# A spectral mixer feeding a squared-ReLU MLP: one scheduling block, ordered by a timeline, around the whole kernel body

## The chip, the cores and the metric

The kernel runs on one core of one Trainium2 chip. The metric is the device time of that core in microseconds (us); 838.69 us is the median of three runs of the kernel before (837.92 to 840.66).

## What is computed

Eight sequences of 3008 rows by 256 columns pass through a spectral layer and then, row by row, through an MLP of width 2048. Cut to what matters:

```python
X = np.fft.rfft(x, axis=1)                      # x: 8 x 3008 x 256
Yr = Xr @ w_r - Xi @ w_i + b_r
Yi = Xr @ w_i + Xi @ w_r + b_i
Y = shrink(Yr, 0.01) + 1j * shrink(Yi, 0.01)    # sign(v) * max(|v| - 0.01, 0)
y = np.fft.irfft(Y, n=3008, axis=1)             # as 24064 rows x 256
r = np.maximum(y @ w_in, 0.0)                   # w_in: 256 x 2048
out = (s * (r * r) + b) @ w_out                 # w_out: 2048 x 256
```

## The kernel before

**The spectral half, one batch at a time.** 3008 is 94 x 32, so each Fourier transform is done in two steps of matmuls with tables. A batch b from 1 to 7 passes four stages, each cut into small units:

- `s1_units` (L619): 16 matmuls by the first table (`A_t`, tile names `psf<-x,A_t`). Each result is copied out of PSUM into `u`, stored to DRAM (`ud`), and read back in another layout (`us`, four loads).
- `s23_units` (L649): 12 rounds of forward table (`fwd_unit`, `psf<-F_t,us`), mixing with the weights (`sum_unit` and `mix_unit`, `W_t` and `W_g`), shrinking on DVE (`shrink`, three operations L714 to L716), moving quarters between partitions (L725, 32 KB DMAs issued by SP, for the last two rounds DVE copies, L727), and the inverse table (`inv_unit`, `psf<-ring,T_t`). The results are copied into `v`, stored to DRAM (`vd`, L744, six stores), and read back as two halves (`vs`, L755).
- `s4_units` (L777): 64 matmuls of 94 columns by the last table (`psf<-C_t,vs`), in 14 groups of up to five. Each group fills one PSUM buffer of the pool `psf` (two buffers) and is copied out by ACT or DVE into `yt` (L187 or L189).

Batch 0 goes through `first_batch` (L409) without the way through DRAM.

**The MLP half, tile by tile.** `yt` is cut into 47 tiles of up to 512 rows (`_tile_order`, L73). For each of the 16 slices of the width, `first_mm` (L851) multiplies by `w_in`; two slices share a double PSUM buffer (`psh`, two of them). ACT applies the ReLU (L871, `rt<-psh`), and ACT or DVE squares it into `gt` (L881 or L884). The product with `w_out` follows one tile later: `second_mms` (L922) with 16 accumulating matmuls per 128 rows, or `seven_mms` (L983), which forms a 2x2 block product from seven products; sums of its operands are made on DVE (`s_op`, L965, L980) and by an accumulating DMA (L973), and DVE combines the results (`add`, L1011 to L1012). Results leave through `ost` by SP's stores.

**What orders the work.** The body emits everything by hand. A dictionary `plan` (L1082 to L1131) gives each unit of the next batches a slot among the 47 x 16 slots of the MLP's loop (L1134 to L1146): in each slot stand the planned units, one `first_mm` and a sixteenth of the previous tile's second product. For instance, stage 4 of batch b is spread over 13 or 14 slots that start 15 (or 14) slots ahead of that batch's own first tile:

```python
        schedule(s2 - 15 + (p < 90), 14 - (p < 90), s4_units(b))
...
                for u in plan.pop(ti * MC + mc, []):
                    u()
                first_mm(ti, mc)
...
            for u in nxt[mc]:
                u()
```

Which of ACT and DVE takes a copy or a square is decided while the body is emitted, by running loads (`evac`, L183; `act_first`, L180). The order in which SP and POOL issue DMAs also follows the emission. In a few places `tc.issue_after` ties instructions to others on their engine.

Of the kernel before, what the change touches and what calls it, by code (L numbers as in the profile page):

```python
# [96 lines left out]
def kernel(  # L97
# [11 lines left out]
    out: bass.AP,  # L109
):  # L110
    nc = tc.nc
    B, S, D = x.shape
    N = S
    assert N == N1 * N2 and D == 2 * P and B % 2 == 0
# [1063 lines left out]
```

## Time and profile before

| | before |
|---|---|
| median of 3 runs | 838.69 us |
| span of the profiled execution | 837.9 us |
| the run nearest to that span | 837.92 us |
| PE busy, share of the span, matmuls | 822.6 us, 98%, 7662 |
| ACT busy | 723.0 us, 86% |
| DVE busy | 706.9 us, 84% |
| POOL busy | 86.2 us, 10% |
| bytes moved by DMA | 107.17 MB, mean 128 GB/s |

The span runs from the first to the last instruction of the program; the execution around it adds next to nothing here. Two things help in reading. A matmul's duration in the trace includes its way through the array, so that neighbours overlap: what a matmul occupies PE for is the distance from its start to the next one's. And a row like `L871 ACT ACTIVATE rt<-psh ... x328 | 336.1, 1026 | 54.4 <-PE psh L175 52.6` says that 328 operations of that form were busy for 336.1 us, 1026 ns each, and that ACT sat idle for 54.4 us ahead of them, 52.6 of these until a matmul into `psh` was done.

### The profile page before, as it was taken

To read this page: it belongs to the slowest core of one execution; us is meant where nothing else is said; L and a number is where in the kernel's file an instruction comes from. 1 tells how busy PE (TensorE), PEld (TensorE's weight loads), DVE (VectorE), ACT (ScalarE), POOL (GpSimd) and SP (SyncE) were. 2 spreads that over 40 slices of the span, in tenths; PEclk is the share of its full clock that TensorE was granted. 3 is DMA by queue.
4 is the path that set the end of the run, shared out by engine and by line. 5 is a ranking of instruction groups with operands and counts; after the bars stand their busy time and mean duration, and the time that the engine had idled before them with its cause. 6 is when DMAs were issued, how large, how long until landed. Compare 5 with 4: busy or idle time off the path is not lost.

```text
span 837.9 us, 19547 instructions
## 1 busy us (share of the span) xinstructions
PE 822.6 (98%) x7662; PEld 600.7 (72%) x7662; DVE 706.9 (84%) x1104; ACT 723.0 (86%) x962; POOL 86.2 (10%) x114
## 2 busy tenths in 40 slices
PE   8999999999999999999999999999999999999997
PEld 7857767777677767777677676767767777767765
DVE  5888989978898888988889888797889988889885
ACT  4998988998899989998889988989889988788882
POOL 4540001100011001100011000100001000001000
PEclk8999999999999999999999999999999999999999
DMA  8954578345873378444773368723565333513321
GB/s 196 180 153 103 124 189 203 63 94 133 198 185 65 94 184 208 114 104 128 195 185 69 88 147 208 175 63 105 127 178 138 67 100 93 137 45 77 72 65 60
DMA packets 116670, 107.17 MB, mean 128 GB/s; under 512 B 12774, under 2 KB 100842, under 8 KB 115234
## 3 DMA queue, kind: packets, MB, share of 16 engines
q1 hardware_dynamic: 102498, 80.55, 33.6%
q0 software_dynamic: 14080, 25.37, 19.1%
q8 instruction: 60, 0.98, 0.5%
q14 instruction: 32, 0.26, 0.1%
HBM read 53.52 MB, written 46.66 MB: 120 GB/s over the span
## 4 chain that ended last, share of the span: by engine, by line
PE 75%; DVE 12%; ACT 6%; DMA 3%; issue 3%; SPq 0%; POOL 0%; DVEq 0%; POOLq 0%
PE psh L175 31%; PE psa L175 28%; PE psf L175 16%; ACT rt L871 3%; DVE gt L884 2%; DVE gt L980 2%; ACT gt L881 1%; DVE ring L699 1%; PE psm L175 1%; DMA gt<-gt 1%; DVE ost L1012 1%; DMA ring<-ring 1%; DVE s L980 1%; DMA x<-in_x_dram 1%; DVE zz L1012 1%
## 5 line engine op out<-in xcount | busy, mean ns | idle before, releaser
L871 ACT ACTIVATE rt<-psh 128x1024 f32<-128x1024 f32 (+2 forms) x384 | 386.7, 1008 | 57.0 <-PE psh L175 55.1
L175 PEld LDWEIGHTS <-gt 128*128 128x128 f16 (+1 forms) x3696 | 304.8, 101 | 167.7 <-DMA gt<-gt 0.5
L175 PE MATMUL psh<-yt,w_in 128*128 128x512 f16 (+1 forms) x1344 | 397.1, 378 | 0.1
L884 DVE TENSOR_TENSOR gt<-rt 128x1024 f16<-128x1024 f32 (+2 forms) x239 | 286.2, 1202 | 78.6 <-ACT rt L871 77.6
L175 PE MATMUL psa<-w_out_t,gt 128*128 128x256 f16 (+3 forms) x2448 | 310.9, 253 | 0.3 <-DMA gt<-gt 0.3
L175 PEld LDWEIGHTS <-w_in 128*128 128x128 f16 x1536 | 136.5, 98 | 24.4 <-issue 1.7
L881 ACT ACTIVATE gt<-rt 128x1024 f16<-128x1024 f32 (+2 forms) x145 | 150.8, 1040 | 3.4
L175 PE MATMUL psa<-T_s,gt 128*128 128x128 f16 (+1 forms) x944 | 79.4, 219 | 0.0
L973 POOL DMA_DIRECT2D gt<-gt x42 | 38.0, 905 | 316.2 <-PE psh L175 66.3
L187 ACT CAST u<-psf 96x512 f16<-96x512 f32 x96 | 55.6, 581 | 9.3 <-PE psf L175 8.6
L699 DVE TENSOR_TENSOR ring<-psf,s 128x512 f16<-128x512 f32 x84 | 57.7, 686 | 3.5 <-PE psf L175 2.5
L187 ACT CAST v<-psf 128x512 f16<-128x512 f32 x79 | 45.8, 583 | 13.6 <-PE psf L175 13.5
L234 POOL DMA_DIRECT2D x<-in_x_dram x36 | 19.2, 539 | 325.1 <-PE psf L175 324.0
L175 PE MATMUL psh<-tail,w_in 128*128 128x512 f16 (+1 forms) x192 | 52.1, 353 | 0.0
L175 PEld LDWEIGHTS <-xf 128*128 128x128 f16 x504 | 46.6, 98 | 6.6 <-DVE xf L672 1.5
L175 PE MATMUL psf<-W_g,xf 128*128 128x256 f16 x336 | 50.4, 272 | 0.0
L187 ACT CAST yt<-psf 128x470 f16<-128x470 f32 (+2 forms) x84 | 43.3, 534 | 3.4 <-PE psf L175 2.2
L1012 DVE SCALAR_TENSOR_TENSOR ost<-psa,s_bc,zz 128x256 f32<-128x256 f32 (+1 forms) x80 | 35.9, 480 | 9.8 <-PE psa L175 8.2
L187 ACT CAST xf<-psf 128x512 f16<-128x512 f32 x64 | 37.4, 585 | 4.2 <-PE psf L175 3.9
L945 DVE SCALAR_TENSOR_TENSOR ost<-psa,s_bc,bias_bc 128x512 f32<-128x512 f32 (+2 forms) x51 | 37.1, 727 | 3.8 <-PE psa L175 1.4
L175 PE MATMUL psf<-x,A_t 94*96 94x512 f16 x102 | 39.0, 382 | 1.4 <-ACT yt L187 0.3
L175 PE MATMUL psf<-C_t,vs 96*128 96x94 f16 (+1 forms) x484 | 37.9, 205 | 0.0
(118 smaller groups left out, 802.6 us busy)
## 6 DMA issues: line engine op xcount, KB each, us to landing
out_dram<-ost SPq DMA_DIRECT2D x152, 128.0 KB
ud<-u SPq DMA_DIRECT2D x56, 192.0 KB
us<-ud SPq DMA_DIRECT2D x28, 384.0 KB
vd<-v SPq DMA_DIRECT2D x42, 256.0 KB
vs<-vd SPq DMA_DIRECT2D x14, 768.0 KB
x<-in_x_dram POOLq DMA_DIRECT2D x28, 376.0 KB, 6.0
gt<-gt POOLq DMA_DIRECT2D x38, 256.0 KB, 4.4
ring<-ring SPq DMA_DIRECT2D x280, 32.0 KB
```

Of the source, the lines that this page charges most:

```text
L175: return nc.tensor.matmul(out, lhs, rhs, **how)
L187: return None, nc.scalar.copy(out=dst, in_=src)
L234: nc.gpsimd.dma_start(out=t[0:N1, i * w : (i + 1) * w], in_=xv[:, c * XCH * D + i * w : c * XCH * D + (i + 1) * w],)
L699: nc.vector.tensor_tensor(out=ring[0][:, i % 4], in0=ps, in1=hold[i // 2][:, i % 2].unsqueeze(1).to_broadcast([P, 2, D]), op=ALU.add,)
L871: nc.scalar.activation(out=rt[:, :, 0:w], in_=ps[:, :, 0:w], func=AF.Relu)
L881: nc.scalar.activation(out=gt, in_=rr, func=AF.Square)
L884: last_square[0] = nc.vector.tensor_tensor(out=gt, in0=rr, in1=rr, op=ALU.mult)
L945: nc.vector.scalar_tensor_tensor(out=ost[0:size, 0:k], in0=ps[0:size, 0:k], scalar=s_bc[0:size], in1=bias_bc[0:size].unsqueeze(1).to_broad ...
L973: nc.gpsimd.dma_start(out=a12, in_=a11, accum_op=ALU.add)
L980: nc.vector.tensor_tensor(out=out, in0=a, in1=b, op=op)
L1012: nc.vector.scalar_tensor_tensor(out=out, in0=of, scalar=s_bc[0:size], in1=other, op0=ALU.mult, op1=ALU.add)
```

## The change

One line is added at the top of the kernel function. From there to the end of the function, all instructions belong to one scheduling block, and the scheduler orders them by a timeline of all of them: an instruction is placed on its engine when, on that timeline, what it needs is there and its buffer is free. Before, they stood in the order of emission. The computation, the buffers and the choice between ACT and DVE are as they were.

```diff
     nc = tc.nc
+    ctx.enter_context(tc.block(schedule_with_timeline_sim=True))
     B, S, D = x.shape
```

The two built programs hold the same instructions (7662 matmuls, 962 operations on ACT, 1104 on DVE, 668 DMAs on SP, 86 on POOL), in another order. On POOL nothing stands more than 4 places from where it stood. On PE the start and the end are alike, and the middle is not. PE's list where batch 2 ends its inverse table and enters stage 4, shortened to output, inputs and count, with "(...)" where rows are left out:

```
before                              after
psf<-ring,T_t           x2          psf<-ring,T_t           x4
psh<-yt,w_in            x2          psa<-T_s,gt             x16
(... psh, psa, some A_t:            psf<-x,A_t              x2
 14.0 us by start-to-start)         psa<-T_s,s1             x16
psh<-yt,w_in            x2          (... psa and A_t: 5.6 us
psf<-C_t,vs             x5           by start-to-start in all)
psa                     x7          psa<-w_out_t,gt         x9
psh<-yt,w_in            x2          psf<-C_t,vs             x64
psf<-C_t,vs             x5          psh<-yt,w_in            x2
(... 14 such groups, spread)        psf<-F_t,us             x4
```

## The prediction

> **What bounds the kernel now.** I read the page's busy rows first, then PE's timeline, to see whether PE is full or only looks full.
>
> ```profile
> PE 822.6 (98%) x7662; PEld 600.7 (72%) x7662; DVE 706.9 (84%) x1104; ACT 723.0 (86%) x962; POOL 86.2 (10%) x114
> PE   8999999999999999999999999999999999999997
> PEclk8999999999999999999999999999999999999999
> ```
>
> PE is busy in every slice but the first and last. The timeline at stage 4 of batch 6 shows how (start, duration, matmuls, count):
>
> ```profile
> 623.66 0.59 PE L175 MATMUL psh<-tail,w_in 128*128 128x512 f16 x2
> 624.09 0.55 PE L175 MATMUL psa<-w_out_t,gt 128*128 128x128 f16 x7
> 624.48 0.37 PE L175 MATMUL psf<-C_t,vs 96*128 96x94 f16 x5
> 624.69 0.60 PE L175 MATMUL psh<-tail,w_in 128*128 128x512 f16 x2
> ```
>
> Start to start, a 512-column matmul takes 0.43 / 2 = 0.215 us, one of 128 columns 0.39 / 7 = 0.056, one of 94 columns 0.21 / 5 = 0.042; of 256 columns, 0.109. Summed over all 7662 matmuls that is 810 us ("PE work" below). The span is 837.9, so 28 us are not stream: 6 ahead of the first matmul and after the last, 22 in gaps, 10 of these in the first 60 us. **PE's stream is the bound, and a new order can win 28 us at the very most.** Every wait that it adds on PE costs its full length.
>
> **What the order does.** I compared the lists of both built programs. Instructions are the same; start and end are nearly the same. In between, `psa` work is taken as soon as it is ready, so it is used up when the next batch's chain is needed. I summed PE work at the seven batch boundaries, from batch b's last inverse matmul (`psf<-ring,T_t`) to its first stage-4 matmul (`psf<-C_t,vs`), and from there to its last one:
>
> ```
> batch               1     2     3     4     5     6     7
> before, to first  17.3  14.0  15.5  14.1  14.0  14.1  12.9
> before, to last   13.8  13.0  12.5  13.3  11.9  13.3  11.9
> after,  to first   1.1   5.6   5.3   6.4   8.1   4.9   6.9
> after,  to last    6.2   2.6   2.6   6.2   2.6   5.1  14.0
> ```
>
> 2.6 us is the 64 matmuls alone: in batches 2, 3 and 5 nothing stands between them.
>
> **Step 1, the load that was hidden.** Between the two stands a chain: copy to `v`, store to `vd`, load of both `vs` halves. Before, for batch 6:
>
> ```profile
> 610.19 0.38 PE L175 MATMUL psf<-ring,T_t 128*128 128x256 f16 x2
> 610.91 0.59 ACT L187 CAST v<-psf 128x512 f16<-128x512 f32 x1
> 611.53 0.38 SPq L744 DMA_DIRECT2D vd<-v  x1
> 612.30 1.35 SPq L638 DMA_DIRECT2D ud<-u  x1
> 614.80 0.79 SPq L755 DMA_DIRECT2D vs<-vd  x2
> ```
>
> From the last matmul (610.29) to the loads' issue are 4.5 us; 3.6 to 8.3 over the batches, mostly 3.6 to 5.8. SP waits there for the store to land. The trace's packets of 8192 bytes (192 of them, both halves) end 7.9 us after the issue here, and 9.3 to 10.3 in batches 2, 4 and 5. Where the halves were issued apart (713.49 and 717.43) the first took about 4. So the first half is there at 4.3 + 4 = 8.3 us after the last inverse matmul, the second at 4.3 + 8.6 = 12.9. I take the middle of the rows, as the same transfers are issued in the same company.
>
> **Step 2, fourteen evictions through two buffers.** Each group of five needs a `psf` buffer, of two:
>
> ```profile
> L187 ACT CAST yt<-psf 128x470 f16<-128x470 f32 x71 | 38.4, 557 | 3.2 <-PE psf L175 2.0
> L175 PE MATMUL psf<-C_t,vs 96*128 96x94 f16 x448 | 34.7, 205 | 0.0
> ```
>
> One buffer's round: 0.21 stream, 0.16 to the end of the last matmul, 0.04 to ACT, 0.557 eviction, 0.05 back: 1.02 us, so 0.51 per group with two buffers. (11 of a batch's 14 evictions are ACT's, which alone would give 0.46.) The last eight groups need the second half: 8 x 0.51 = 4.1. A boundary thus lasts 12.9 + 4.1 = **17.0 us**, unless PE has as much to do. Before it had 24.8 to 31.1 everywhere, so all was hidden. After, PE has the sum of the two lower rows: 7.3, 8.2, 7.9, 12.6, 10.7, 10.0, 20.9. Lost: 9.7 + 8.8 + 9.1 + 4.4 + 6.3 + 7.0 + 0 = **45.3 us**. Bounds: 3.6 + 7.9 + 8 x 0.46 = 15.2 gives 34; 5.8 + 10.3 + 4.1 = 20.2 gives 65. The next batch's `us` loads (four, behind `vs` in SP's queue) start in this pause and land inside it; PE's first use of them stands behind all 64 matmuls, so I cost them at nothing. If the pause were gone they would be late next.
>
> **Step 3, restart.** With `psa` used up, PE's only work after the boundary is `psh`, which follows ACT:
>
> ```profile
> L871 ACT ACTIVATE rt<-psh 128x1024 f32<-128x1024 f32 x328 | 336.1, 1026 | 54.4 <-PE psh L175 52.6 <-PE psf L175 1.2
> ```
>
> Back to back such a ReLU takes 0.92 us (in ACT's timeline one starts at 610.00 and the next operation at 610.91), and evictions and squares stand between. After batch 3, PE reaches its 13th `psh` pair with 17.7 us of work, but needs the 11th ReLU, which ends at 1.1 (first pair) + 18.2 (ACT's work ahead of it) + 0.92 = 20.2: 2.5 us lost. Worked so, the seven boundaries lose 3.0, 1.3, 2.5, 2.5, 1.1, 2.5, 1.1 = **14.0 us** (7 to 20).
>
> **Step 4, DVE in the drain.** Ahead of boundaries 1, 2 and 3 DVE's additions (L980, L1012) are packed more densely than PE's work: DVE's work grows by 10.3, 6.8 and 8.4 us more than PE's between waits, by at most 5.2 elsewhere. The order before has such a growth of 5.1 and no wait with it, and the median slack of such a wait is 5.5; less 5.5 each: 4.8 + 1.3 + 2.9 = **9.0 us** (0 to 20).
>
> **Step 5, the clock.** PE's granted clock fell once before, behind a start with pauses (windows: length, busy of PE, PEld, DVE, ACT, POOL, then PEclk):
>
> ```profile
> 7.92 0.50 PE L175 MATMUL psm<-A_t,x 94*128 94x96 f16 x4 [1.51 <-DMA x<-in_x_dram]
> ...
> 7.70:14.60 6.90, 6.68 (x74) 6.46 (x75) 3.21 (x14) 3.87 (x9) 1.47 (x2) 0.51 0.93 173
> 14.60:20.00 5.40, 5.28 (x66) 4.59 (x64) 4.50 (x13) 3.70 (x8) 1.30 (x4) 1.00 0.85 287
> ```
>
> Half clock held for 6.8 us. Six boundaries with longer pauses may each bring it: up to 3.4 us of stream each, much of it inside step 3's wait for ACT. I take 1.5 each, **9 us** (0 to 20). The Trainium skill, "TensorE: Matmul & The Clock Gate", section "What's actually happening", has the gate go to half rate after an idle window of about 3.4 us, and back after one busy window; by that every pause of steps 1 and 2 drops the clock, and my estimate from its figure is 1.7 us per boundary, so 10 instead of 9. This trace agrees that it drops, but held it for 6.8, twice that window.
>
> **What may be won.** PE's waits for DVE's results, one at each of four boundaries before:
>
> ```profile
> PE psa L175 <- DVE ost L1012: 4.5, 8, 0.9
> ```
>
> About **4 us** (0 to 12, all gaps after the first 60 us).
>
> **Sum** on the profiled execution: 837.9 + 45.3 + 14.0 + 9.0 + 9 - 4 = 911.2 us. The median of the runs is 0.8 above that span: **912 us**.
>
> **The rivals.**
>
> - *The loads land before PE arrives* (chance 0.10). Then only step 2 is left: 14 x (0.51 - 0.21) = 4.2 us at batches 1, 2, 3 and 5 and half of it at 4 and 6, 21 us: 838.7 + 21 = 860. It needs loads within some 5 us of the last inverse matmul; the rows give 8.3 and more.
> - *Taking work as soon as it is ready keeps PE fed, and the time falls* (0.04). The mechanism: `psh` runs further ahead, so ReLU and square are long done when `psa` wants them; in the new order the median slack of PE's waits on ACT and DVE, chain alone, is 3.1 us against 2.2. It would remove the 12 us of gaps after the first 60 us: 838.7 - 12 = 827. It decides only if the boundaries have 17 us of PE work; they have 7.3 to 12.6 at six of seven. The lists speak against it in another way too: waits on ACT and DVE whose chain alone is longer than PE's work since its producer are 23 before (2.9 us in sum) and 133 after (65 us, with double counting where two buffers take turns), 65 of them in stage 4.
> - *ACT and DVE trail in the middle as well* (0.06): they are 86% and 84% busy and their new order rests on a timeline that isn't the chip. PE's waits on them rise from 649 to 851 and from 403 to 536. With steps 1, 3, 4 and 5 at their upper bounds: 838.7 + 65 + 20 + 20 + 20 = 964.
> - *The change does nothing*: out, since the lists differ.
>
> **Numbers.** The forecast case has 0.80. Lower end of the range, all lower bounds with the largest gain: 838.7 + 34 + 7 - 12 = 868. Upper end 950, short of 964, where all upper bounds meet. Of the first rival's 0.10, 0.02 is for loads and evictions so well placed that nothing is left to measure. Faster by over 0.3% (which is about what a measurement of this kernel tells from no change): 0.04; within: 0.02; slower: 0.94.
>
> **What would show it.** PE's busy tenths with dips near 17%, 29%, 41%, 53%, 64% and 76% of the span (PE work at the boundaries plus what is lost ahead of them); the waits view with PE or PEld waiting for DMA `vs<-vd` or for ACT `yt`, neither of which is of size now; 14 evictions `yt<-psf` in about 7 us; PEclk below 9 behind the dips; PE's start-to-start sum still 810. I am wrong if C_t's 64 matmuls run within 3 us, or if PE's gaps stand between the boundaries and not at them.

## The result, and the profile after

| | before | after |
|---|---|---|
| median | 838.56 us (4 runs, 837.92 to 840.66) | 998.24 us (4 runs, 993.33 to 1000.6) |
| ratio, 95% interval | | 1.188 (1.185 to 1.191) |
| span of the profiled execution | 837.9 us | 996.8 us |

Slower, as forecast, but by 159.7 us where the forecast said 73, and outside the range (868 to 950). The profiled execution took 998.61 us, 1.8 more than its span. The page after, busy rows, PE's tenths and clock:

```profile
PE 875.0 (88%) x7662; PEld 624.4 (63%) x7662; DVE 702.7 (70%) x1104; ACT 720.5 (72%) x962; POOL 84.1 (8%) x114
...
PE   8999973699964999579996899969999799989996
...
PEclk9999996799995999769999999979999799999999
```

A slice is 2.5% of the span. PE dips at 15%, 30%, 41%, 53%, 66% and 78%: six of the seven batch boundaries, near the six places forecast. The clock falls in or just behind most dips. ACT and DVE do what they did (720.5 and 702.7 us busy), in a longer span. The waits view (engine, line, tile <- releaser: us in sum, times, longest; lines stand one lower, L176 for L175):

```profile
PEld L176 <- DMA vs<-vd: 36.5, 7, 14.5
...
PE psf L176 <- DMA vs<-vd: 33.6, 7, 13.7
...
PEld L176 <- DMA gt<-gt: 23.9, 12, 8.0
PE psa L176 <- DMA gt<-gt: 20.9, 8, 7.7
...
PEld L176 <- DMA ring<-ring: 10.4, 2, 8.8
```

None of the three was of size before. The load of `vs` was foreseen; the accumulating DMA (`gt<-gt`, L974) and the moves between partitions (`ring<-ring`, L726) were not; two of those were waited for, 8.8 us at batch 1 and 1.6 at batch 2. (PE and PEld wait at the same time; the two are not added.)

To see where the 159 us went, I took each matmul's distance to the next start, less its usual one (0.215 us for 512 columns and so on, twice that where the granted clock was half). What is left is idle PE; the extra of the half clock is counted apart. Per stage of a boundary, all seven together, us:

```
                                              idle PE       half clock
                                            before after   before after
25 us ahead of the last inverse matmul        1.5   23.1     0     5.6
last inverse matmul to first C_t              0.1   63.4     0     2.7
stage 4, first C_t to last                    2.1   25.2     0    13.1
25 us behind it                               2.4   21.9     0     8.7
all the rest                                 14.4   15.5    3.0    1.4
sum                                          20.5  149.1    3.0   31.5
```

Idle time grew by 128.6 and the half clock's cost by 28.5: 157.1 of 158.9 us. **Between the boundaries almost nothing changed** (15.5 us of idle PE against 14.4). Batch 3's boundary in the timeline, first SP's queue, then PE (its last inverse matmul started at 409.02):

```profile
409.94 0.44 SPq L745 DMA_DIRECT2D vd<-v  x1
410.98 1.14 SPq L639 DMA_DIRECT2D ud<-u  x1
420.82 0.79 SPq L756 DMA_DIRECT2D vs<-vd  x2
```

```profile
426.33 0.97 PE L176 MATMUL psf<-C_t,vs 96*128 96x94 f16 x10 [5.67 <-DMA vs<-vd]
427.55 1.00 PE L176 MATMUL psf<-C_t,vs 96*128 96x94 f16 x10 [0.25 <-ACT yt L188]
428.73 1.42 PE L176 MATMUL psf<-C_t,vs 96*128 96x94 f16 x11 [0.18 <-ACT yt L188]
431.35 0.89 PE L176 MATMUL psf<-C_t,vs 96*128 96x94 f16 x9 [1.19 <-DMA vs<-vd]
```

SP waited from 412 to 420.82 for the store to land. The first half is there 5.5 us after that, the second 5.0 later. At batch 2 PE met the accumulating DMA in the same stretch, and afterwards the late `us` load:

```profile
308.90 1.11 PE L176 MATMUL psa<-w_out_t,gt 128*120 128x128 f16 x8 [7.73 <-DMA gt<-gt]
...
321.39 0.61 PE L176 MATMUL psf<-F_t,us 128*128 128x128 f16 x4 [2.54 <-DMA us<-ud]
```

The clock around batches 2 and 3 (windows: length, busy of PE, PEld, DVE, ACT, POOL, then PEclk, DMA share, GB/s):

```profile
301.00:324.90 23.90, 12.45 (x91) 8.24 (x90) 3.90 (x8) 7.67 (x14) 1.49 (x2) 0.50 0.72 194
324.90:335.10 10.20, 9.74 (x69) 6.02 (x68) 5.57 (x9) 10.07 (x13) 0.00 (x0) 1.00 0.00 1
417.10:441.00 23.90, 14.09 (x93) 8.74 (x94) 3.90 (x8) 9.29 (x16) 1.47 (x2) 0.50 0.81 216
```

Half clock held for 23.9 us, well past the pauses of 7.7 us (batch 2) and 5.7 us (batch 3); PE is busy for 52 and 59% of that time only.

### The profile page after: what moved, and what is told of

It reads as the page before. It is cut to its first block, busy times and chain, and to the rows that moved or that the text cites. A ratio compares the mean times of both kernels' runs of the same rounds, so it can differ in the third digit from the quotient of the medians.

```text
span 996.8 us, 19608 instructions
## 1 busy us (share of the span) xinstructions
PE 875.0 (88%) x7662; PEld 624.4 (63%) x7662; DVE 702.7 (70%) x1104; ACT 720.5 (72%) x962; POOL 84.1 (8%) x114
## 5 line engine op out<-in xcount | busy, mean ns | idle before, releaser
L176 PEld LDWEIGHTS <-gt 128*128 128x128 f16 (+1 forms) x3696 | 300.3, 103 | 110.1 <-DMA gt<-gt 23.9
L176 PE MATMUL psh<-yt,w_in 128*128 128x512 f16 (+1 forms) x1344 | 353.5, 385 | 8.3 <-ACT rt L872 7.8
L176 PE MATMUL psa<-w_out_t,gt 128*128 128x256 f16 (+3 forms) x2448 | 287.0, 257 | 26.8 <-DMA gt<-gt 20.9
L176 PEld LDWEIGHTS <-w_in 128*128 128x128 f16 x1536 | 146.4, 99 | 115.1 <-issue 23.6
L882 ACT ACTIVATE gt<-rt 128x1024 f16<-128x1024 f32 (+2 forms) x145 | 154.2, 1078 | 1.4
L176 PE MATMUL psa<-T_s,gt 128*128 128x128 f16 (+1 forms) x944 | 84.7, 223 | 1.8 <-DVE ost L1013 1.0
L176 PE MATMUL psf<-C_t,vs 96*128 96x94 f16 (+1 forms) x484 | 44.8, 251 | 44.3 <-DMA vs<-vd 33.6
L974 POOL DMA_DIRECT2D gt<-gt x42 | 38.3, 918 | 486.6 <-PE psh L176 201.5
L176 PEld LDWEIGHTS <-vs 96*128 96x128 f16 x512 | 37.2, 124 | 55.0 <-DMA vs<-vd 36.5
L176 PEld LDWEIGHTS <-xf 128*128 128x128 f16 x504 | 48.6, 98 | 25.1 <-issue 6.0
L190 DVE CAST yt<-psf 128x470 f16<-128x470 f32 (+2 forms) x23 | 12.5, 544 | 63.0 <-PE psf L176 62.8
L176 PE MATMUL psf<-W_g,xf 128*128 128x256 f16 x336 | 50.5, 273 | 2.6 <-DVE ring L700 1.4
L176 PE MATMUL psh<-tail,w_in 128*128 128x512 f16 (+1 forms) x192 | 44.9, 359 | 1.6 <-ACT rt L872 1.4
```

The costliest lines, as they stand in the source:

```text
L176: return nc.tensor.matmul(out, lhs, rhs, **how)
L190: return nc.vector.tensor_copy(out=dst, in_=src), None
L882: nc.scalar.activation(out=gt, in_=rr, func=AF.Square)
L974: nc.gpsimd.dma_start(out=a12, in_=a11, accum_op=ALU.add)
```

## The experiments

The kernel before took 838.8 to 839.7 us beside them. **The theory:** PE's new order takes second-product work (`psa`) as soon as it is ready, nothing is left to cover the chain `v`, `vd`, `vs` at a boundary, and that chain is longer than I took it to be. **The rivals:** the block itself or the order on the other engines costs the time; the accumulating DMA alone costs it; the chain merely had too low a priority.

### Which part of the new order

**The block without the timeline.** The program's lists are those of before.

```diff
+    ctx.enter_context(tc.block())
```

> The body in one block, but without the timeline: on every engine the list of instructions is the one of before. Theory (PE pauses where the order lets MLP matmuls overtake the next batch's spectral chain): 838 to 840 us. Rival (the block itself costs, by its entry or its waits): clearly above, 850 or more.

Measured: 839.34 us, ratio 0.9995 (0.998 to 1.0005). The block costs nothing; the order is all.

**PE in the order of emission, the other engines by the timeline.**

```diff
+        with tc.issue_after(last_mm[0].ins):
+            mm = nc.tensor.matmul(out, lhs, rhs, **how)
+        last_mm[0] = mm
```

> The timeline block, with each matmul tied behind the one emitted before it. PE's list is that of before to 0.3 places on average, and with it the other engines' lists (0.05 to 0.35 places). Theory: 836 to 843 us. Rival (what the timeline does to ACT, DVE and SP costs by itself): it would show as a part of the 160 us only if those lists still differed; with lists this near, over 850 would speak for waits that the lists do not show.

Measured: 846.92, ratio 1.009 (1.006 to 1.012), a little above the expectation. The boundaries idle 10 us in all. Holding PE's order removes 151 of the 160 us. Since the other engines' lists fall back with it (to within 0.35 places), the run shows what PE's order and all that follows from it are worth, and not PE's order alone.

**The reverse: ACT, DVE, SP and POOL in the order of emission, PE free.**

> The timeline block, with ACT, DVE, SP and POOL tied to the order of emission and PE free. PE's list differs from that of before by 27 places on average (after: 111), but at the seven boundaries PE has 26 to 34 us of work between the last inverse matmul and the last of stage 4, more than the 17 us that the chain takes. Theory: no pauses there, 838 to 850 us. Rival (any order of PE that is not the emission's costs, in proportion to how far it moves): 838 + 160 x 27 / 111 = 877 us.

Measured: 940.54, ratio 1.120 (1.118 to 1.123): missed by far, for both theories. Between last inverse matmul and first `C_t` only 2.2 us are idle, and the half clock costs 3.2, so what I said of the boundary held there. But 120 us of idle time stand all over the span:

```profile
PE psh L207 <- ACT rt L110: 25.1, 60, 1.0
...
PEld L207 <- DMA gt<-gt: 17.1, 13, 2.5
...
PEld L207 <- DVE gt L110: 14.3, 33, 1.0
```

(The operations of the pinned engines pass through one helper, L110.) Many short waits for the ReLU and the squares: a free PE order beside pinned engines has a loss of its own. From the lists I would argue that PE work between a `psh` pair and the first `psa` that reads its square, 5.7 us in the median before, is 3.7 here, so that any queue on ACT or DVE reaches PE. No run isolates that.

**One half of the MLP tied.** In the changed kernel, a slot's first MLP matmul is put behind the spectral units that were emitted ahead of it.

```diff
+                if units:
+                    last_unit[0] = last_mm[0]
+                with tc.issue_after(last_unit[0].ins):
+                    first_mm(ti, mc)
```

> The timeline block with one tie: each first MLP matmul of a slot stands behind the spectral units that were emitted ahead of it, so the MLP can't overtake the chain; all else is the timeline's. PE's list differs from that of before by 38 places on average; at the boundaries PE has 25 to 29 us of work. Theory: 838 to 855 us. Rival (disorder costs in proportion): 838 + 160 x 38 / 111 = 893 us.

Measured: 878.24, ratio 1.046 (1.044 to 1.048), between theory and rival. This one tie takes away 120 of the 160 us; idle time from last inverse to first `C_t` falls from 63.4 to 6.9. The 57 us of idle PE that are left are spread (the squares, some 10, the accumulating DMA, 7.5, `vs`, 6.6), as in the run before this. No run isolates what the 39 us that stay over the kernel before are due to.

**The other half tied:** the slot's second product behind its first MLP matmul.

```diff
+                with tc.issue_after(last_first[0].ins):
+                    for u in nxt[mc]:
+                        u()
```

> The changed kernel with the other half of the MLP tied: the second product's matmuls of a slot stand behind the slot's first MLP matmul on PE, while the first MLP matmuls may still run ahead of the spectral units. By PE's list 1.1 to 3.5 us of work stand between the last inverse matmul and the first C_t in batches 1 to 6 (7.5 in batch 7) and stage 4 is in a row. Theory (the cover is used up by the first MLP matmuls that run ahead, and with them all that follows; where the tie leaves the boundary's list as it is, the loss stays): 960 to 1020 us, waits for vs<-vd 50 us or more over PE and PEld. Rival (it is the second product, most of the MLP's work, that runs ahead; a tie between it and its slot brings back most of the 160 us, as the other tie did): 850 to 900 us.

Measured: 976.67, ratio 1.165 (1.162 to 1.169): the theory. So it is the first MLP matmuls that must not run ahead of the spectral units. With them gone early, the rest of the MLP is gone too, and the boundary is bare:

```profile
PEld L176 <- DMA vs<-vd: 64.0, 8, 13.7
PE psf L176 <- DMA vs<-vd: 57.8, 8, 12.8
```

**The spectral units at high priority.**

```diff
-                for u in plan.pop(ti * MC + mc, []):
-                    u()
+                with tc.high_priority():
+                    for u in plan.pop(ti * MC + mc, []):
+                        u()
```

> The changed kernel with every planned unit (the stages of the spectral half, the loads of x and us) emitted at high priority, so that where the timeline has both ready, the scheduler takes the spectral instruction ahead of the MLP's. By PE's list it moves instructions by some ten places only, and 1 to 10 us of other PE work stand between the last inverse matmul and the first C_t, as in the changed kernel. Theory (the order never lets PE stand idle on its timeline, so that the MLP's work which the hand order kept back as cover is used up before the chain's end arrives; no priority brings it back): 980 to 1010 us, waits for vs<-vd 50 us or more in sum over PE and PEld. Rival (the chain was only served late, at too low a priority): the first C_t comes with the chain's shortest time of some 8 us and the waits for vs<-vd fall below half, time 880 to 940 us.

Measured: 991.76, ratio 1.181 (1.178 to 1.184): the theory. Priority decides among what is ready; it keeps nothing back.

### The accumulating DMA

`s_op` number 4 as an addition on DVE instead of a DMA, first in the kernel before (the control), then in the changed one.

```diff
-        if n == 4:
-            nc.gpsimd.dma_start(out=a12, in_=a11, accum_op=ALU.add)
-            return
+            4: (a12, a12, a11, ALU.add),
```

> Control: the same replacement in the kernel before, where PE waits 0.6 us for those DMAs. Both theories: 838 to 846 us; DVE goes from 707 to some 736 us of busy time.

> The changed kernel with the accumulating DMA of the seven-product tiles (POOL, 42 of them) replaced by a DVE addition. In the changed kernel's trace PE waits 23 us for those DMAs. Theory (these waits are a pause of their own, ahead of the wait for the load): about 998 - 23 - some 5 of half clock = 970 us, with 29 us more of DVE work. Rival (the pause only moves to the next late thing, the load of vs or DVE): 993 to 1003 us.

Measured: 844.94 in the control (1.006, 1.005 to 1.008), 978.11 with the change (1.165, 1.163 to 1.167), so 20.1 us less than the changed kernel although the control loses 5. The waits for `gt<-gt` (23.2 us by the distances) are gone, those for `vs` grew from 34.8 to 46.8, and the half clock's cost fell from 31.5 to 21.9. The DMA is a real term of the loss, partly in place of waiting for `vs`; it is not the cause of it.

### The boundary rebuilt by hand

These change the order written out in the kernel before, with no timeline. First only the bunching: all 14 groups of stage 4 in one slot, long after the loads have landed.

```diff
-        schedule(s2 - 15 + (p < 90), 14 - (p < 90), s4_units(b))
+        schedule(s2 - 2, 1, s4_units(b))
```

> The kernel before with all 14 groups of stage 4 in one slot, two slots ahead of the batch's first tile, long after the loads have landed (18 us or more of PE work stand between). Only batches 2 to 7. Theory: PE has 6.1 to 6.8 us of work for a stretch that two buffers let pass in 7.1, and ReLUs come late behind 11 evictions on ACT: 1 to 4 us per boundary, 845 to 865 us. Rival (bunching itself carries the loss, 8 us and more per boundary with the clock): 885 us or more.

Measured: 859.26, ratio 1.024 (1.022 to 1.025). Idle time in stage 4 is 12.0 us, behind it 13.0; the stage lasts 8.2 to 8.9 us from first to last `C_t` (I had 7.1); the clock stays full. This is the theory's range; bunching alone does not carry the loss. Then the inverse table up to 20 slots later as well, so that some 8 us of PE work are left between the last inverse matmul and the first `C_t`:

```diff
-        schedule(s1 + 2, p - 30, units)
-        plan.setdefault(s2 - 23, []).append(take_half)
+        schedule(s1 + 2, p - 10, units)
+        plan.setdefault(s2 - 7, []).append(take_half)
```

> The kernel before with stage 4 bunched as in the run on bunching, and the inverse table some 15 slots later: PE has 7.3 to 8.4 us from the last inverse matmul to stage 4, 5.1 to 6.7 from there to its end, 13 to 15 in all against the chain's 17, in batches 2 to 7. The second products are still spread as before. Theory: 2 to 4 us more per boundary than the bunched run, and some half clock: 858 to 890 us. Rival (the pause at the chain is not what costs; it is the used-up second products): as the bunched run, within 5 us.

Measured: 910.61, ratio 1.085 (1.084 to 1.087), above the expectation. By my 8.3 us the first half should have been there; PE waited 36.4 us at six boundaries. SP's queue at batch 2 (start, duration of the issue):

```profile
236.33 4.37 SPq L644 DMA_DIRECT2D us<-ud  x3
240.80 2.17 SPq L744 DMA_DIRECT2D vd<-v  x1
247.38 0.79 SPq L755 DMA_DIRECT2D vs<-vd  x2
```

The last `vd` is issued behind three `us` loads of 384 KB, and `vs` 6.6 us later. To test whether this company lengthens the chain, I moved the loads by slot:

```diff
-        for q, at in enumerate((-9, -6, -1, 4)):
+        for q, at in enumerate((1, 2, 4, 8)):
```

> The kernel of the late bunch (910.6 us, 36 us of waits of PE for vs<-vd in batches 2 to 6, stage 4 in one slot behind about 8 us of other PE work) with one thing moved: the four us loads of the next batch (384 KB each) are issued from one slot behind the batch's start instead of from nine slots ahead of it, and its forward rounds begin four slots later. PE's list at the boundary stays: 7.3 to 8.2 us of work from the last inverse matmul to the first C_t. Theory (the chain of v, vd, vs is 15 to 17 us long there because the vd store and the vs loads share SP's queue and the DMA engines with the us loads): from the issue of the last vd to the issue of vs falls from 6.3 to 7.1 us to 2.4 to 4 us, the first C_t stands 9 to 12 us behind the last inverse matmul, the waits for vs<-vd fall to 5 to 18 us, the time to 876 to 895 us. Rival (the store's way to DRAM and the two halves are that slow whatever else is under way): waits for vs<-vd stay at 30 us or more, time 902 to 918 us.

Measured: 908.76 (1.083, 1.080 to 1.085). That test failed and tells nothing of the chain: SP still issued the loads ahead of the last `vd`, though they were now emitted behind it. (So the order of DMAs on SP does not simply follow the emission, as the section on the kernel before has it.) It does show that the later forward rounds alone change nothing (908.76 against 910.61). With the loads tied behind `vs` (the forward rounds begin four slots later, as in the run before this):

```diff
+                with tc.issue_after(vs_load[1].ins) if b > 2 else ExitStack():
+                    nc.sync.dma_start(out=t, in_=uv[:, 6 * q : 6 * q + 6, :])
```

> The edit that the run before this one did not bring onto the queue (in its trace SP still issued the us loads of the next batch ahead of the last vd store): now the four us loads are tied behind the second vs load of the batch, and SP's list has vd, vs, vs, us, us, us, us. PE's list at the boundaries stays as in the late bunch (7.3 to 8.0 us of work from the last inverse matmul to the first C_t). Theory (the us loads on SP's queue and in the DMA engines lengthen the chain of v, vd, vs): from the issue of the last vd to that of vs falls from 6.3 to 7.1 us to 2.4 to 4 us, the first C_t stands 9 to 12 us behind the last inverse matmul in batches 2 to 6, PE's waits for vs<-vd fall from 36 us to 5 to 18, the time from 910 to 876 to 895 us. Rival (the way through DRAM is that slow whatever else is under way): waits for vs<-vd of 30 us or more, 902 to 918 us.

Measured: 879.73, ratio 1.048 (1.046 to 1.050): the theory. Waits before, then with the tie:

```profile
PEld L175 <- DMA vs<-vd: 36.6, 6, 8.3
...
PE psf L175 <- DMA vs<-vd: 35.4, 6, 8.1
```

```profile
PEld L175 <- DMA vs<-vd: 14.5, 7, 3.0
...
PE psf L175 <- DMA vs<-vd: 12.8, 6, 2.8
```

SP's queue at batch 2 with the tie:

```profile
232.54 5.30 SPq L746 DMA_DIRECT2D vd<-v  x2
241.00 0.79 SPq L757 DMA_DIRECT2D vs<-vd  x2
241.84 1.49 SPq L646 DMA_DIRECT2D us<-ud  x2
```

In batches 2 to 6 `vs` is now issued 2.6 to 3.8 us after the last `vd` (6.4 to 7.1 without the tie), and the first `C_t` comes 9.9 to 11.9 us after the last inverse matmul instead of 14.9 to 17.3. Of these 5.1 us in the mean, 1.7 are the last `vd` issued sooner, and 3.4 are the way from its issue to that of `vs`. From the issue of `vs` to the first `C_t` nothing changed: 5.4 to 6.1 us in both. **The same store comes out later and lands later where other transfers are queued ahead of it; the loads behind it take as long as before.** The tie is worth 29 us of the kernel's time (31 against the late bunch). The Trainium skill, "DMA: Bandwidth & Descriptors", section "Queues, rings and completion order", says that the marker of completion is written only after every earlier write of that DMA engine, across queues; the measured delay of the store agrees, but does not tell this from shared bandwidth.

## Why the prediction was wrong

The direction, the cause (PE's work taken early) and the place (seven boundaries, nothing between) were right, and the runs with tied matmuls show the cause. The sizes were not. The growth against before, from the table above:

- *Steps 1 and 2, the bare chain and stage 4*: 45.3 forecast, 86.4 measured. **Step 1 failed first.** It has the first half of `vs` there 8.3 us after the last inverse matmul: 4.3 to the issue of `vs` plus 4 for one half. Measured, the first `C_t` started 9.7 to 22.5 us after the last inverse matmul, 15.0 in the mean. `vs` was issued 4.1 to 11.8 us after it (mean 7.1), because the store lands later (2.4 to 10.9 us from its issue to that of `vs`). The first `C_t` stands 5.5 to 13.6 us behind that issue, not 4. The 13.6, at batch 2, is the accumulating DMA: PE waited 19.9 us for such DMAs in these two stretches, and the forecast had no term for them. But even in the late bunch with the `us` loads tied it stands 5.5 to 6.1 us behind, since half of the packets need 4.2 to 4.5 us and PE starts 1.1 to 1.7 later.
- *Where the trace of before had it*: there `vs` was issued 4.9 us after the last inverse matmul in the mean, and all its packets were in 9.8 us after the issue, where I took 4.3 and 8.6. Half of them were in at 8.2 to 14.5 us, mean 10.5, hidden under 13 to 17 us of work. I priced one half by a case where it travelled alone, and that by 4 where its packets end 4.5 us after the issue; at batch 3, the other case of halves issued apart, half of the packets needed 6.3. And I took the middle of quiet rows for boundaries that would not be quiet.
- *Step 2 by itself* was the smaller miss: stage 4 lasted 7.9 to 12.2 us in six batches, with half clock and other work of PE in it, where the forecast leaves 8.7 (17.0 less 8.3); the bunched kernel, with nothing to load, shows 8.2 to 8.9. Batch 7 was set to no loss, since 20.9 us of work are more than 17.0; but the work behind the first `C_t` cannot cover a wait ahead of it, and 4.5 us were lost there.
- *The `us` loads at nothing*: 3.3 us of waits, small.
- *Step 3, restart behind the ReLU*: 14.0 forecast, 19.5 measured, 3.3 of it those `us` loads. 11.1 us of this stretch's idle time stand ahead of `psh` matmuls, which need the ReLU: the size is about right. The mechanism is not shown: the bunched kernel, whose second products are not used up, loses 13.0 behind stage 4 as well, but only 4.4 of that ahead of `psh`.
- *Step 4, DVE in the drain*: 9.0 forecast, 21.6 measured. Only 5.9 of it are waits for DVE's results (7.1 more stand in the next stretch); 10.1 are the two waits for `ring<-ring` DMAs (8.7 at batch 1, 1.4 at batch 2), which I had not looked at.
- *Step 5, the clock*: 9 forecast, 28.5 measured. I let half clock end with one window of 6.8 us and let six pauses bring it. It came eleven times after the start and held for 3.4 to 23.9 us, while stage 4 and the restart kept PE thin. "0 to 20" ended too low.
- *The gain of 4*: nothing; the gaps elsewhere are 15.5 against 14.4.

Sum: 86.4 + 19.5 + 21.6 + 28.5 + 1.1 = 157.1 us. Of the rivals, none came: the loads were late rather than early, PE was not fed better, and the middle does not trail with all engines on the timeline's order. That last one did appear where PE alone was free. The terms are also not independent, as I had summed them: without the accumulating DMA, the waits for `vs` grew by 12.0 us and the half clock's cost fell by 9.6.

What stays open: how much of the store's late landing in the changed kernel (SP's waits for it are 24.3 us in sum, 8.6 the longest) is due to which neighbour. There the `us` loads stand behind `vs` already, and an `x` load, `ud` stores and the accumulating DMAs are under way; no run took these away one by one. And no order tried here beats the kernel before.

## What to carry to other kernels

An order that never lets the busiest engine stand idle on its timeline spends the work that a hand order keeps back to cover the next long chain; look for what is kept back, and tie it where it is needed, since priority did not hold it here. Price an exposed DMA chain by its slowest rows with company, not by a quiet one, and count every DMA whose result the engine reads in that stretch. Half clock is a cost of thin work as well as of pauses: price it by the length of the thin stretch.

## What the runs showed of the hardware

- Half clock outlasts the pause that brought it: 23.9, 23.9 and 20.5 us at three boundaries, in which PE was busy for 38 to 59% of the time, and full again afterwards (0.95 busy at 324.9 to 335.1). The Trainium skill, "TensorE: Matmul & The Clock Gate", section "What's actually happening", lets it return after one sustained busy window of about 3.4 us; this trace agrees as far as such a window only came later: the first 3.4 us with PE busy throughout ended 3.4 us ahead of the return at all three.
- Half clock needs no pause of 3.4 us: thin work is enough. Cut into the trace's steps of 3.4 us, the changed kernel fell to half clock only behind steps with PE busy for at most 50%, and stayed at full clock behind every step above that (in two other runs it fell behind steps of 57 and 58%). At 290.8 the longest pause in the step before was 1.0 us (PE busy for 1.69 of 3.40 us), at 403.4 it was 1.8 us (1.26 of 3.40). The one drop of the kernel before, at 7.7 us, was already of this kind: in the window ahead of it PE was busy for 1.49 of 3.40 us at full clock, and its longest pause was the 1.51 us that the prediction shows.

```profile
4.30:7.70 3.40, 1.49 (x25) 1.14 (x22) 0.56 (x1) 0.48 (x1) 1.73 (x4) 1.00 1.04 208
```

- Two loads of 768 KB issued together land half of their packets 4.5 to 8.8 us after the issue and all of them 8.7 to 14.3 after it (changed kernel). In the late bunch with the `us` loads tied, half are in after 4.2 to 4.5 us, no later than the one that travelled alone (4.5, batch 7 before). So the second load did not hold up the first there; which of the other transfers does so in the changed kernel, no run isolates.
